# Gated attention and two feed-forward stages on one core: the first 384 tokens' feed-forward runs its first two steps before the second 384 tokens' attention begins

## The chip, the core and the metric

The kernel runs on one core of a Trainium2 chip. What is measured is device time in microseconds (us) from the start of the program to its end. The core has TensorE (PE in the profile) for matrix products, VectorE (DVE), ScalarE (ACT) and GpSimd (POOL) for work on tiles, and SyncE (SP), which here only issues DMA transfers. Each engine works through its own list of instructions in order and waits at an instruction until what that instruction needs is there.

## What is computed

A gated recurrence over 768 tokens (4 sequences, 8 heads of 48), then a product of two linear maps, then a choice of one of eight experts for each token:

```python
for t in range(S):                                   # attention
    state = alpha[:, :, t, :, None] * state + k_t v_t^T
    y[:, :, t] = q_t @ state
x = y as 3072 tokens x 384                           # first feed-forward stage ("moe")
x = ((x @ w_a) * (x @ w_b)) @ w_out                  # 384 -> 1536 -> 384
e = argmax(x @ w_gate + modality_bias[modality_id])  # second stage ("moe2")
out = gate(e) * (relu(x @ w1[e]) @ w2[e])            # 384 -> 1024 -> 384
```

All inputs but the modality ids are float64 or float32 with float32 accuracy wanted; the weights arrive as 64-bit numbers.

## The kernel before, in words

The 3072 tokens are cut into 8 groups of 384 (`WIN`), each of three chunks of 128. For each group `Attention` makes `xh[w]` and `xl[w]`: the attention output transposed and split into a high and a low part, so that a product is three fast passes on TensorE. `moe(w)` then takes the group through the first feed-forward stage in 12 steps f of 128 hidden columns: 9 products into `ab0` and 9 into `ab1` (L625), ScalarE copies the first (`asb`, L630), VectorE multiplies (`g`, L632), ScalarE and VectorE split it into `gh` (L634) and `gl` (L638), and one step later 9 products with `w_out` gather in three banks `px` (L616).

The weights come as 64-bit words and are turned into float32 parts by `convert`. They are loaded in six slices r = 0 to 5 (`load_weights(r)`: `wa`, `wb`, `wo`, each 768 KB, on SP's queue), and each slice serves two steps f. To convert one slice of one weight takes VectorE four instructions on 128x768 elements: L181, L184 and L188 put a float32 together in `cva`, `cvb` or `cvo`, then ScalarE writes the high part (L192) and VectorE the low part (L196) into `pa`, `pb` or `po`. `weights()` does them in the order a0, b0, o0, a1 and b1, o1, a2 and b2, and so on.

All this must happen beside the first group, since later groups use the converted weights again. So the beginning of the kernel is this: the attention of group 0 (`first`, an order written out by hand, with eight conversion instructions in it), then the 12 steps of `moe(0)`, and beside them the conversion of the slices and the attention of group 1 (`later`, `att1`). In this part the order on VectorE and SP is the program's order (`manual_schedule`), and the string `SEQ` says what that is: `r` is the next conversion step (one instruction of VectorE, with ScalarE's where there is one), `m` the first half of a step f, which ends with `gh`, `n` its second half with `gl` and the products of the step before, and `a` the next step of group 1's attention. Of these, `prepare(c)` has three: (1) the clamp of the turned alpha, a scan over it and a reciprocal (L370, L379, L382), (2) `kt` (L388), (3) a second scan and `qt` (L390, L392). Then come the scores (L404 on TensorE), the mask (L421, L422), `values` and `halves` (L452 to L479, with `xl` at L479), and the state's update (L509). TensorE, ScalarE and GpSimd take their order from a planner.

Turning (`turn`, L343) is a transpose of a raw tile on TensorE; alpha, k and q of a chunk are `raw_a`, `raw_k`, `raw_q`, loaded at L325. The turned tiles lie in three banks of PSUM until `prepare` has read them. On SP's queue group 1's first raw tiles go out ahead of `wo` of slice 0 and all of slice 1; a transfer waits until the eighth one before it has landed.

Of the kernel before, what the change touches and what calls it, by code (L numbers as in the profile page):

```python
# [29 lines left out]


SEQ = (
    "rrrmrrnaaarrrmrnrarra" "rrrmrrnaarrrmrnrarra" "rrrmrrnaarrrmrnrarra" "rrrmrrnaarrrmrnrarra" "rrrmrrnaarrrmrnrarr"
    "rrrmrnmnm"
)
WARM0, WARM1 = 7, (0, 3, 4, 0, 3, 0, 0, 0, 1)
# [8 lines left out]
def gla_moe_kernel(ctx, tc, q, k, v, alpha, w_a, w_b, w_out, modality_id, w_gate, modality_bias, w1, w2, out):  # L45
    nc = tc.nc
# [96 lines left out]
    words, parts, newest = {}, {}, {}  # L143
# [8 lines left out]
    def load_weights(r, names="abo"):  # L152

        for nm, w in (("a", w_a), ("b", w_b)):
            if nm not in names:
                continue
            words[nm, r] = new_w(f"w{nm}{r}", I32)


            heads = w.bitcast(I32)[:, r * 512 : (r + 1) * 512].rearrange("(h d) f -> h d f", h=H)  # L160
            for i in range(4):
                nc.sync.dma_start(  # L162
                    out=words[nm, r][32 * i : 32 * i + 32, : 2 * 512].rearrange("p (k f) -> p k f", k=2),
                    in_=heads[i::4, :32].rearrange("k d f -> d k f"),
                )
            nc.sync.dma_start(out=words[nm, r][:, 2 * 512 :], in_=heads[:, 32:])
        if "o" not in names:
            return
        words["o", r] = new_w(f"wo{r}", I32)
        newest["w"] = nc.sync.dma_start(  # L170
            out=words["o", r].rearrange("p (f d) -> p f d", f=2),
            in_=w_out.bitcast(I32)[r * 2 * P : (r + 1) * 2 * P, :].rearrange("(f p) d -> p f d", p=P),
        )
# [72 lines left out]
                    return  # L246
            yield

    def behind(steps):

        while True:
            with tc.issue_after(newest["mm"].ins):
                try:
                    next(steps)
                except StopIteration:
                    return
            yield
# [24 lines left out]
    class Attention:  # L282
# [206 lines left out]
        def carry(self, c):  # L489
            ktok = self.ktok.pop(c)  # L490
            pu = self.bank(f"u{self.w}_{c}")
            for p in range(NPAIR):
                nc.tensor.matmul(  # L493
                    pu[:, p * 96 : (p + 1) * 96],
                    ktok[:, p * P : (p + 1) * P],
                    self.vt[c][:, 2 * p : 2 * p + 2, :].rearrange("p h d -> p (h d)"),
                    start=True,
                    stop=True,
                )
            self.pu[c] = pu  # L500
# [277 lines left out]
    def small(name, shape, dt=F32):  # L778
        return m2.tile(shape, dt, bufs=1, name=name)
# [375 lines left out]
    def pipeline(y_d=None):  # L1155
        nonlocal ap, m2, fold, starts
        nc.vector.tensor_copy(base, eoff)
        with tc.tile_pool(name="att", bufs=1) as ap:
            if y_d is None:
                starts = ap.tile([P, NPAIR * P1], F32, name="starts")  # L1160
                nc.gpsimd.memset(starts, 0.0)

            def weights():
                yield from convert(0, "a", P)
                yield from convert(0, "b", P)
                for r in range(NF // 2):
                    o = convert(r, "o", DM)
                    yield from islice(o, 3)
                    ab = convert(r + 1, "ab", P) if r + 1 < NF // 2 else iter(())
                    yield from islice(ab, 1)  # L1170
                    yield from o
                    yield from ab

            if y_d is None:
                with tc.manual_schedule(engines={EN.DVE, EN.PE, EN.SP, EN.Activation}):
                    att0 = Attention(0, (nc.sync, nc.scalar))
                    for c, which in ((0, "akq"), (1, "akq"), (0, "v"), (2, "akq"), (1, "v"), (2, "v")):
                        att0.load(c, which)
                    rest = weights()
                    load_weights(0, "ab")  # L1180
                    later = Attention(1)

                    def second():
                        later.load(0, "akq")
                        load_weights(0, "o")
                        later.load(0, "v")
                        load_weights(1)

                    att0.first(rest, second)
                with tc.manual_schedule(engines={EN.DVE, EN.SP}):  # L1190
                    att1 = later.steps()
                    next(att1)
                    load_weights(2)
                    clear_table()
                    nc.sync.dma_start(out=wg_sb, in_=w_gate.rearrange("(k p) e -> p k e", p=P))
                    load_weights(3)
                    g0 = dict(r=rest, m=moe(0), a=att1)
                    f, done = 0, 8
                    g0["n"] = g0["m"]
                    for c in SEQ:  # L1200
                        if c == "m":
                            assert not (f < NF and ("b", f // 2) not in parts or f > 1 and ("o", f // 2 - 1) not in parts)
                            f += 1
                        done += c == "r"
                        if c == "r" and done == 14:
                            load_weights(4)
                            load_weights(5)
                        next(g0[c], None)
                    run((g0["m"], 1), (rest, 8), (att1, 1))
                    run((load_ids(), 1))  # L1210
                for w in range(1, NW - 1):
                    if w == 1:
                        with tc.issue_after(newest["mm"].ins):
                            turn_gate()
                        gate = gate_columns("gate", ap, 2, tag="cv", bufs=4)
                    att = Attention(w + 1)
                    run((after_first(att.steps()) if w == 1 else att.steps(), RATIO), (moe(w), 1), (route(w - 1, ap, gate if w > 2 else None), 1))
            else:
                for r in range(NF // 2):
                    load_weights(r)  # L1220
                clear_table()
                run((weights(), 1))
                for w in range(NW - 1):
                    x_from(w, y_d)
                    run((moe(w), 1))
                    if w < NW - 2:
                        run((route(w, ap), 1))
                x_from(NW - 1, y_d)
        with tc.tile_pool(name="m2", bufs=2) as m2:
            fold = small("fold", [P, TINY])  # L1230
            nc.vector.tensor_reduce(fold, ident.rearrange("p (j c) -> p c j", c=TINY), axis=AX.X, op=ALU.add)
            last = moe(NW - 1)
            gate = gate_columns("last", m2, 4, tag="wr", bufs=6) if y_d is None else None
            run((islice(last, 1), 1))
            early = []
            run((islice(last, MIX[0]), 1), (behind(chain(route(NW - 2, m2, gate), early_table(early))), 2))
            slots = [Slot(f"e{i}", "e", i, 2, (NW - 1) * WIN) for i in range(NEARLY)]
            for s_ in slots:
                s_.index()
            for s_ in slots[:2]:  # L1240
                s_.load()
            run((islice(last, MIX[1]), 1))
            if y_d is None:
                run((behind(spans()), 1))
            with tc.manual_schedule(engines=VECS):
                run((last, 1), (slots[0].split(), SPLIT), (behind(pause(MIX[2], slots[0].rows())), 1))

            big, tiny = [("l", i, 2) for i in range(NSB)], [("r", XSMALL + i, 1) for i in range(NTINY + XTINY)]
            order, rest = big[:NBIG], [big[NBIG:], [("r", i, 1) for i in range(XSMALL)], tiny[NTINY:]]
            riders = {}  # L1250
            if y_d is None:
                riders = {RIDE[n]: Tiny(f"t{n}", *tiny[n][:2], N) for n in range(NTINY)}
            else:
                order, rest = big + rest[1] + tiny, []
            slots += [Slot(f"l{n}", *o, N) for n, o in enumerate(order)]
            with nullcontext() if rest else tc.manual_schedule(engines={EN.SP}):
                puts = []
                go(slots, 1, (route(NW - 1, m2, puts=puts), early[0], puts), riders)
        return rest
# [108 lines left out]
    rest = pipeline()  # L1368
# [37 lines left out]
```

## Time and profile before

| what | us |
|---|---|
| median of 3 runs | 896.39 |
| lowest and highest of them | 895.86 and 898.45 |
| profiled execution, device time | 897.17 |
| its span, first to last instruction | 895.2 |
| VectorE busy in the span | 636.0 (71%) |
| TensorE busy in the span | 840.8 (94%) |

The profiled execution's own time is 0.78 us over the median. The share of the whole span says little here: the change touches only the stretch from some 25 us to 120 us after the start, in which VectorE is the busiest engine after TensorE. Times in the rows below are counted from the start of the span.

### The profile page before, as it was taken

How to read it: one execution, taken by the hardware profiler on the slowest of the kernel's cores; microseconds unless marked ns; L12 is line 12 of the kernel's file. 1: busy time of each engine (PE TensorE's matmuls, PEld its weight loads, DVE VectorE, ACT ScalarE, POOL GpSimd, SP SyncE). 2: the span in 40 equal slices, each digit the busy share in tenths (PEclk: the TensorE clock that was granted, in tenths of full speed). 3: DMA queues.
4: the chain of work that ended last, by engine and by line, in shares of the span. 5: the costliest groups of instructions: out<-in, count | busy, mean ns of one | idle time of the engine just before them, and what ended most of it. 6: DMA issues, size and time to landing. Idle time of an engine off the chain costs nothing.

```text
span 895.2 us, 16751 instructions
## 1 busy us (share of the span) xinstructions
PE 840.8 (94%) x6220; PEld 786.0 (88%) x6220; DVE 636.0 (71%) x1457; ACT 292.1 (33%) x681; POOL 199.5 (22%) x273
## 2 busy tenths in 40 slices
PE   7888889988997999999999999999699999999995
PEld 6677789978996999989899998999699999998994
DVE  7699889964595788499698676366369876775751
ACT  2223332212221222212122122122265555565541
POOL 5011101120011101011100100000425565455431
PEclk9889999998998999999999999999899999999998
DMA  9999846332234214023220000210580988695810
GB/s 170 200 197 199 181 123 207 93 62 68 63 77 74 81 28 106 27 63 96 41 78 10 1 28 1 71 28 1 202 299 24 361 289 310 191 358 186 281 60 22
DMA packets 124928, 110.98 MB, mean 124 GB/s; under 512 B 55759, under 2 KB 104051, under 8 KB 124836
## 3 DMA queue, kind: packets, MB, share of 16 engines
q1 hardware_dynamic: 114548, 99.00, 40.7%
q0 software_dynamic: 4032, 9.62, 3.1%
q10 hardware_dynamic: 6256, 1.19, 1.1%
q8 instruction: 51, 0.84, 0.4%
q14 instruction: 41, 0.34, 0.1%
HBM read 100.10 MB, written 9.82 MB: 123 GB/s over the span
## 4 chain that ended last, share of the span: by engine, by line
PE 65%; DVE 12%; DMA 10%; issue 6%; SPq 3%; POOL 2%; ACT 2%; POOLq 0%; DVEq 0%; ACTq 0%
PE ab L625 24%; PE px L616 12%; PE hl L1056 8%; PE pol L1004 8%; DMA wa<-in_moe_w_a 3%; PE he L1056 2%; PE s L404 2%; PE poe L1004 2%; DMA wb<-in_moe_w_b 2%; DMA tab_d<-rec,posi 2%; PE u L493 1%; DVE g L632 1%; DMA raw_a<-in_alpha 1%; SPq L162 1%; DVE at L358 1%
## 5 line engine op out<-in xcount | busy, mean ns | idle before, releaser
L625 PE MATMUL ab<-xh,pb 128*128 128x384 f32 x576 | 168.8, 346 | 16.3 <-DVE g L632 16.3
L625 PE MATMUL ab<-xh,pa 128*128 128x384 f32 x576 | 167.4, 344 | 9.7 <-ACT asb L630 7.3
L616 PE MATMUL px<-po,gh 128*128 128x384 f32 x576 | 139.5, 342 | 3.4 <-ACT gh L634 3.1
L634 ACT ACTIVATE gh<-g 128x384 fp32r<-128x384 f32 x96 | 50.3, 524 | 240.4 <-DVE g L632 234.4
L625 PEld LDWEIGHTS ab<-xh,pb 128*128 128x128 f32 x576 | 107.5, 191 | 21.4 <-DVE g L632 18.3
L625 PEld LDWEIGHTS ab<-xh,pa 128*128 128x128 f32 x576 | 106.2, 190 | 14.0 <-ACT asb L630 7.9
L632 DVE TENSOR_TENSOR g<-ab,asb 128x384 f32<-128x384 f32 x96 | 53.0, 552 | 81.5 <-PE ab L625 75.6
L616 PEld LDWEIGHTS px<-po,gh 128*128 128x128 f32 x576 | 104.3, 191 | 5.5 <-ACT gh L634 4.1
L625 PE MATMUL ab<-xl,pb 128*128 128x384 f32 x288 | 98.0, 340 | 0.0
L625 PE MATMUL ab<-xl,pa 128*128 128x384 f32 x288 | 97.4, 338 | 0.0
L630 ACT ACTIVATE asb<-ab 128x384 f32<-128x384 f32 x96 | 47.0, 490 | 147.8 <-PE ab L625 147.5
L616 PE MATMUL px<-po,gl 128*128 128x384 f32 x288 | 87.0, 341 | 0.0
L638 DVE TENSOR_TENSOR gl<-g,gh 128x384 fp32r<-128x384 f32 x96 | 56.2, 586 | 21.6 <-ACT gh L634 21.3
L392 POOL TENSOR_TENSOR qt<-qt,at 128x512 f32<-128x512 f32 x18 | 22.3, 1237 | 220.8 <-DVE qt L358 168.3
L1061 DVE SCALAR_TENSOR_TENSOR hll<-hl,hhl 128x256 fp32r<-128x256 f32 x72 | 30.3, 421 | 54.1 <-ACT hhl L1059 53.7
L671 DVE SCALAR_TENSOR_TENSOR junk<-xr,gate 128x384 bf16<-128x384 f32 x96 | 54.0, 562 | 4.8 <-ACT xr L648 3.2
L625 PEld LDWEIGHTS ab<-xl,pb 128*128 128x128 f32 x288 | 55.1, 191 | 0.1
L625 PEld LDWEIGHTS ab<-xl,pa 128*128 128x128 f32 x288 | 54.7, 190 | 0.1
L732 POOL DMA_INDIRECT tab_d<-rec,posi x24 | 24.2, 1010 | 135.7 <-DMA tab_d<-rec,posi 67.0
L616 PEld LDWEIGHTS px<-po,gl 128*128 128x128 f32 x288 | 52.9, 189 | 1.0 <-issue 0.6
L1059 ACT ACTIVATE hhl<-hl 128x256 fp32r<-128x256 f32 x72 | 27.7, 384 | 61.8 <-PE hl L1056 56.5
L437 POOL TENSOR_TENSOR state<-state,R 128x384 f32<-128x384 f32 x18 | 17.5, 971 | 131.2 <-DVE state L509 62.8
(332 smaller groups left out, 1860.0 us busy)
## 6 DMA issues: line engine op xcount, KB each, us to landing
w1rl<-in_moe_w SPq DMA_DIRECT2D x18, 768.0 KB, 8.1
w2rl<-in_moe_w SPq DMA_DIRECT2D x18, 768.0 KB, 4.9
raw_a<-in_alpha SPq DMA_DIRECT2D x72, 96.0 KB, 2.3
raw_k<-in_k SPq DMA_DIRECT2D x72, 96.0 KB, 2.3
raw_q<-in_q SPq DMA_DIRECT2D x72, 96.0 KB, 2.7
wo<-in_moe_w_out SPq DMA_DIRECT2D x6, 768.0 KB, 7.9
x_d<-xr SPq DMA_DIRECT2D x24, 192.0 KB, 2.1
w1re<-in_moe_w SPq DMA_DIRECT2D x6, 768.0 KB, 14.3
```

Source lines behind the costliest of these rows:

```text
L616: newest["mm"] = nc.tensor.matmul(px[t][:, :DM], a_, b_, start=(f == 0 and i == 0), stop=(f == NF - 1 and i == 2))
L625: nc.tensor.matmul(pt[:, :WIN], a_, b_, start=(n == 0), stop=(n == 3 * KD - 1))
L630: nc.scalar.activation(asb, pt[:, :WIN], AF.Copy)
L632: nc.vector.tensor_tensor(g, pab[1][:, :WIN], asb, op=ALU.mult)
L634: newest["act"] = nc.scalar.activation(gh, g, AF.Copy)
L638: newest["gl"] = nc.vector.tensor_tensor(gl, g, gh, op=ALU.subtract)
L671: nc.vector.scalar_tensor_tensor(junk, xr[w][t], 1.0, gate[e], op0=ALU.mult, op1=ALU.mult, accum_out=L[:, t, e : e + 1])
L732: put = nc.gpsimd.indirect_dma_start(out=tab_d[:, :], out_offset=bass.IndirectOffsetOnAxis(ap=posi[:, t : t + 1], axis=0), in_=rec[:, i, : ...
L1004: newest["mm"] = nc.tensor.matmul(self.po[t][:, :DM], a_, b_, start=(f == 0 and i == 0), stop=(f == NF2 - 1 and i == 2))
L1056: nc.tensor.matmul(pt[:, :n], a_, b_, start=(i == 0), stop=(i == 3 * KD - 1))
L1059: nc.scalar.activation(gh[:, :n], pt[:, :n], AF.Relu)
L1061: nc.vector.scalar_tensor_tensor(gl[:, :n], pt[:, :n], 0.0, gh[:, :n], op0=ALU.max, op1=ALU.subtract)
```

## The change

Three edits. `SEQ` gets a new first piece without any `a`: the first two steps f and the whole conversion of slice 1 (`a1`, `b1` and the first steps of `o1`) come before group 1's attention. The attention starts beside step f = 2; its later pieces hold a step more, so that it is through at the same place, step f = 9. `behind(att1, newest["first"])` makes the planner issue what belongs to group 1's attention behind the last state product of group 0 (L493, third chunk). And slices 4 and 5 are asked for in the program after the third `a` instead of the sixth `r`.

```diff
 SEQ = (
-    "rrrmrrnaaarrrmrnrarra" "rrrmrrnaarrrmrnrarra" ...
+    "rrrmrrnrrrmrnrrr" "rrrmrrnaaarrrmrnrarra" "rrrmrrnaarrrmrnrarra" ...
...
-    def behind(steps):
+    def behind(steps, ins=None):
         while True:
-            with tc.issue_after(newest["mm"].ins):
+            with tc.issue_after((ins or newest["mm"]).ins):
...
             for p in range(NPAIR):
-                nc.tensor.matmul(
+                newest["first"] = nc.tensor.matmul(
                     pu[:, p * 96 : (p + 1) * 96],
...
-                    g0 = dict(r=rest, m=moe(0), a=att1)
-                    f, done = 0, 8
+                    g0 = dict(r=rest, m=moe(0), a=behind(att1, newest["first"]))
+                    f, done = 0, 0
                     g0["n"] = g0["m"]
                     for c in SEQ:
...
-                        done += c == "r"
-                        if c == "r" and done == 14:
+                        next(g0[c], None)
+                        done += c == "a"
+                        if c == "a" and done == 3:
                             load_weights(4)
                             load_weights(5)
-                        next(g0[c], None)
```

The number of instructions stays; SP's list keeps its order. Three places show what moves. In the names the first number is the chunk or step and the last one is a serial number; `y_2` and `u_2` are group 0's third chunk, `pa_0`, `pk_0`, `pq_0` group 1's first turned tiles.

TensorE, end of group 0's attention, before:

```order
L236 MATMUL warm<-ones_b 128x256
L343 MATMUL pa_0_628<-ident,raw_a_0_363 128x128 x4
L343 MATMUL pk_0_641<-ident,raw_k_0_366 128x128 x4
L343 MATMUL pq_0_649<-ident,raw_q_0_369 128x128 x4
L452 MATMUL y_2_497<-qt_2_344,state 64x128 x4
L464 MATMUL y_2_497<-qt_2_344,state 32x128 x4
L468 MATMUL y_2_497<-sm_2_445,v_2_183 32x128 x8
L473 MATMUL y_2_497<-sm_2_445,vpad_116 32x128 x8
L493 MATMUL u_2_522<-v_2_183,ktok_2_443 128x96 x4
```

and after:

```order
L236 MATMUL warm<-ones_b 128x256
L452 MATMUL y_2_497<-qt_2_344,state 64x128 x4
L464 MATMUL y_2_497<-qt_2_344,state 32x128 x4
L468 MATMUL y_2_497<-sm_2_445,v_2_183 32x128 x8
L473 MATMUL y_2_497<-sm_2_445,vpad_116 32x128 x8
L493 MATMUL u_2_522<-v_2_183,ktok_2_443 128x96 x4
L343 MATMUL pa_0_723<-ident,raw_a_0_363 128x128 x4
L343 MATMUL pk_0_736<-ident,raw_k_0_366 128x128 x4
L343 MATMUL pq_0_744<-ident,raw_q_0_369 128x128 x4
```

The three turnings have moved behind the last products of group 0's attention.

VectorE, between the first step f and the conversion of slice 1 (`cva_622`, `cvb_623`), before:

```order
L196 TENSOR_TENSOR po_590<-cvo_586,po_590 128x2x384
L638 TENSOR_TENSOR gl_0_621<-g_0_617,gh_0_619 128x384
L370 TENSOR_SCALAR at_0_627<-pa_0_628 128x4x128
L376 MEMSET R_0_635 128x2
L378 MEMSET starts 128x4
L379 SCALAR_TENSOR_TENSOR R_0_635<-at_0_627,starts 128x516
L382 RECIPROCAL starts<-R_0_635 128x4
L388 TENSOR_TENSOR kt_0_640<-pk_0_641,R_0_635 128x512
L390 SCALAR_TENSOR_TENSOR at_0_627<-at_0_627,starts 128x516
L392 TENSOR_TENSOR qt_0_648<-pq_0_649,at_0_627 128x512
L181 TENSOR_SCALAR cvb_623<-wb_382 128x768
L184 SCALAR_TENSOR_TENSOR cva_622<-wa_376,cva_622 128x768
```

and after:

```order
L196 TENSOR_TENSOR po_590<-cvo_586,po_590 128x2x384
L638 TENSOR_TENSOR gl_0_621<-g_0_617,gh_0_619 128x384
L181 TENSOR_SCALAR cvb_623<-wb_382 128x768
L184 SCALAR_TENSOR_TENSOR cva_622<-wa_376,cva_622 128x768
L184 SCALAR_TENSOR_TENSOR cvb_623<-wb_382,cvb_623 128x768
L632 TENSOR_TENSOR g_1_652<-ab_1_1_642,asb_1_640 128x384
L188 SCALAR_TENSOR_TENSOR cva_622<-wa_376,cva_622 128x768
L638 TENSOR_TENSOR gl_1_656<-g_1_652,gh_1_654 128x384
```

The eight instructions of `prepare(0)` have left this place (they now stand behind `gl_2`), and the conversion that reads `wb` of slice 1 follows `gl_0` directly.

VectorE, where group 1's first chunk is split (`xl_198<-y_0`), before:

```order
L188 SCALAR_TENSOR_TENSOR cvb_799<-wb_560,cvb_799 128x768
L390 SCALAR_TENSOR_TENSOR at_1_752<-at_1_752,starts 128x516
L392 TENSOR_TENSOR qt_1_872<-pq_1_873,at_1_752 128x512
L196 TENSOR_TENSOR pa_856<-cva_798,pa_856 128x6x128
L196 TENSOR_TENSOR pb_869<-cvb_799,pb_869 128x6x128
L479 TENSOR_TENSOR xl_198<-y_0_884,xh_197 128x3x128
```

and after:

```order
L188 SCALAR_TENSOR_TENSOR cvb_894<-wb_578,cvb_894 128x768
L479 TENSOR_TENSOR xl_198<-y_0_977,xh_197 128x3x128
L196 TENSOR_TENSOR pa_959<-cva_893,pa_959 128x6x128
L196 TENSOR_TENSOR pb_972<-cvb_894,pb_972 128x6x128
L509 TENSOR_TENSOR state<-u_0_1013,state 64x4x32
```

`xl` of the first chunk now follows the last of the joins (L188) at once; four instructions that stood between them are elsewhere. From `xl` of the third chunk on, in step f = 9, both lists are the same.

## Rows read from the trace of the kernel before

**Rows 1.** The page's head: span of the profiled execution.
```profile
span 895.2 us, 16751 instructions
```

**Rows 2.** Busy time by stretch; us, busy us of PE, PEld, DVE, ACT, POOL, clock, DMA share.
```profile
28.99:34.78 5.79, 5.34 (x57) 3.89 (x56) 0.00 (x1) 0.49 (x1) 0.00 (x0) 0.50 1.05 262
...
41.12:49.49 8.37, 3.79 (x18) 2.99 (x18) 6.96 (x12) 1.64 (x3) 0.83 (x1) 0.97 1.04 196
49.49:61.59 12.10, 11.86 (x81) 10.48 (x82) 11.89 (x19) 3.57 (x6) 2.40 (x3) 0.74 0.90 203
61.59:119.53 57.94, 51.16 (x388) 45.14 (x388) 52.84 (x81) 22.30 (x42) 5.55 (x8) 1.00 0.88 193
...
130.00:170.00 40.00, 39.52 (x286) 36.77 (x288) 37.41 (x78) 10.72 (x27) 4.95 (x7) 1.00 0.55 160
```

**Rows 3.** VectorE in order of time: start, length, instruction, [idle before it, its releaser].
```profile
34.78 0.56 DVE L479 TENSOR_TENSOR xl<-y,xh 128x384 fp32r<-128x384 f32 x1 [5.79 <-ACT xh L478]
...
36.12 0.55 DVE L181 TENSOR_SCALAR cvo<-wo 128x768 int32<-128x768 int32 x1
...
41.12 0.56 DVE L632 TENSOR_TENSOR g<-ab,asb 128x384 f32<-128x384 f32 x1 [0.83 <-PE ab L625]
...
43.39 0.96 DVE L196 TENSOR_TENSOR po<-cvo,po 128x768 fp32r<-128x768 f32 x1 [1.24 <-ACT po L192]
...
44.73 0.68 DVE L370 TENSOR_SCALAR at<-pa 128x512 f32<-128x512 f32 x1
...
49.49 0.55 DVE L181 TENSOR_SCALAR cvb<-wb 128x768 int32<-128x768 int32 x1
...
53.50 1.39 DVE L188 SCALAR_TENSOR_TENSOR cvb<-wb,cvb 128x768 int32<-128x768 int32 x1
...
56.98 0.68 DVE L370 TENSOR_SCALAR at<-pa 128x512 f32<-128x512 f32 x1
...
59.15 0.53 DVE L181 TENSOR_SCALAR cvo<-wo 128x768 int32<-128x768 int32 x1
...
61.59 0.55 DVE L632 TENSOR_TENSOR g<-ab,asb 128x384 f32<-128x384 f32 x1
```

**Rows 4.** Transfer of `wo`, slice 0, issued at 29.32: KB, us to landing.
```profile
wo<-in_moe_w_out SPq DMA_DIRECT2D x1, 768.0 KB, 5.9
```

**Rows 5.** The chain that ended last, in order of time: start, length, what.
```profile
38.19 7.76 DMA wb<-in_moe_w_b
...
45.97 3.53 DMA wb<-in_moe_w_b
49.50 0.55 DVE cvb L181
...
52.85 2.29 PE px L616 x6
...
56.90 3.15 PE ab L625 x18
```

**Rows 6.** TensorE in order of time, around its gap at 46 to 49 us.
```profile
45.03 0.69 PE L616 MATMUL px<-po,gl 128*128 128x384 f32 x3
49.63 2.08 PE L404 MATMUL s<-qt,kt 64*128 64x128 f32 x16 [3.91 <-DVE qt L392]
```

**Rows 7.** TensorE alone by stretch: us, busy us (instructions), granted clock, DMA share.
```profile
43.50:49.60 6.10, 2.02 (x10) 0.95 1.03 195
49.60:55.80 6.20, 6.07 (x30) 0.50 0.82 190
```

**Rows 8.** VectorE's four waits of over 0.25 us between 62 and 120 us.
```profile
78.33 0.96 DVE L196 TENSOR_TENSOR po<-cvo,po 128x768 fp32r<-128x768 f32 x1 [0.88 <-ACT po L192]
...
101.29 0.67 DVE L638 TENSOR_TENSOR gl<-g,gh 128x384 fp32r<-128x384 f32 x1 [0.31 <-ACT gh L634]
...
104.79 0.56 DVE L479 TENSOR_TENSOR xl<-y,xh 128x384 fp32r<-128x384 f32 x1 [1.96 <-ACT xh L478]
...
119.53 0.56 DVE L479 TENSOR_TENSOR xl<-y,xh 128x384 fp32r<-128x384 f32 x1 [1.29 <-ACT xh L478]
```

More of the change, by code (lines that the diff above doesn't have):

```diff
@@ L32 @@
 SEQ = (
-    "rrrmrrnaaarrrmrnrarra" "rrrmrrnaarrrmrnrarra" "rrrmrrnaarrrmrnrarra" "rrrmrrnaarrrmrnrarra" "rrrmrrnaarrrmrnrarr"
+    "rrrmrrnrrrmrnrrr" "rrrmrrnaaarrrmrnrarra" "rrrmrrnaaarrrmrnrarra" "rrrmrrnaaarrrmrnrarra" "rrrmrrnaaarrrmrnraarra"
     "rrrmrnmnm"
```

## The prediction

> **What bounds the kernel now.** I read the busy time by stretch first, then VectorE's own order of time, then the chain of waits. The page's head gives the span [rows 1]; the profiled execution took 897.17 us, 0.78 us over the median, so I make the sum on 897.17 and take 0.78 off at the end. The edits touch the stretch from about 29 to 120 us. From 61.59 to 119.53 us VectorE is busy 52.84 of 57.94 us and TensorE 51.16 [rows 2]: VectorE has hardly any slack there, and what reaches its list late stays late. Its order from `xl` of the third chunk on (119.53) is that of before, and behind it, from 130 to 170 us, TensorE is busy 39.52 of 40 us and VectorE 37.41 [rows 2], so a delay at 119.53 is carried to the end one to one. The sum is therefore VectorE's lateness at that point.
>
> Ahead of 61.59 VectorE loses time at three places. From 28.99 to 34.78 it waits 5.79 us for `xh`, since TensorE stood at the turnings for raw tiles still on their way and then worked at half clock [rows 2, 3]. It waits 0.83 us before `g` at 41.12 and 1.24 us before `po` at 43.39 [rows 3]. These are what the change could win. From 44.73 to 61.59 it has no idle time: `prepare(0)` (44.73 to 49.49), the conversion of `wb` and `wa` with step 1 (49.49 to 56.98), the first part of `prepare(1)` (56.98 to 59.15), three instructions on `cvo` (59.15 to 61.59) [rows 3].
>
> **Part 1: the turnings behind the products.** TensorE no longer stands at the turnings, so `xl` can begin up to 5.79 us earlier, at 28.99 [rows 3]. What stood between its start and `cvo` L181 took 36.12 - 34.78 = 1.34 us, so VectorE is at `cvo` L181 by 30.3. But this instruction reads `wo` of slice 0, issued at 29.32, landing 5.9 us later, at 35.2 [rows 4]. The transfers do not move: SP's order is the same, its issues wait for earlier landings and not for the engines, and the DMA share in these stretches is 0.90 to 1.05 [rows 2]. So of 5.79 us only 36.12 - 35.2 = 0.9 us is won here; `g_0` and `po` follow some 0.9 us earlier, or up to 0.83 more if the wait for TensorE shrinks too [rows 3].
>
> **Part 2: conversion of slice 1 ahead of prepare(0).** Before, `prepare(0)` began at 44.73 when `gl_0` was through [rows 3]; now `cvb` L181 stands there, ready about 43.8 (44.73 less 0.9). It reads `wb` of slice 1. The last piece of that was issued at 38.19, and the chain shows SP's next issue released 7.76 us later, at 45.95, by this landing [rows 5]. VectorE so sits idle some 2.2 us to 45.95. Everything else in its list is the same work in another order, so the lateness is 45.95 - 44.73 = **+1.2 us**. Bounds: the wait before `cvb` is not in the trace; the landing may come half a microsecond to either side, 0.7 to 1.7. `prepare(0)`'s 4.76 us, which covered this transfer, no longer does. `prepare`'s own cost is not changed, nor that of the instruction that runs longer beside a GpSimd mask (1.39 us at 53.50 [rows 3]): it goes elsewhere with the mask, counted at nothing; at best it is saved, about 0.4 us.
>
> **Part 3: TensorE's clock.** In the trace TensorE ends `px` at 45.72, idles 3.91 us for `qt` and then runs at a granted clock of 0.50 (1.2 GHz) from 49.60 to 55.80, against 0.95 in the stretch with the gap [rows 6, 7]. That cost nothing, since VectorE had 12 us of work by itself. After the change the gap lies in the same place and what follows it is on the path. `px` ends about 44.8 (0.9 earlier). In the chain `px` of step 1 follows `cvb` L181 by 52.85 - 49.50 = 3.35 us, by way of `g_1` and `gh_1` [rows 5], so it now starts at 45.95 + 3.35 = 49.3. The gap is 4.5 us, longer than 3.91, so I expect half clock again for about 6.2 us, to 55.5. Step 1's nine products at 2.29 us for six [rows 5] take 3.4 us, to 52.7. Then the 18 products `ab_2`: 3.15 us at full clock [rows 5], but to 55.5 only 1.4 us of that is done; the rest ends at 57.25. VectorE wants `g_2` after nine instructions from `cvb` on (49.49 to 56.98, 7.5 us, less at most 0.9 for slow ones [rows 3]) and three on `cvo` (2.44 us [rows 3]): 45.95 + 6.6 + 2.44 = 55.0. So it stalls 2.25 us. With TensorE at full clock all the while there is no stall: `px` takes 1.7 us, and `ab_2` can end by 54.7, its last nine waiting for `pb`. Where in the stretch the clock comes back is not fixed by these rows (55.80 is the latest at which it did), so between 0 and 2.25 I take **+1.6**, nearer to the row.
>
> The Trainium skill, in "TensorE: Matmul & The Clock Gate", section "Part 1: The HAM clock gate", says that the low clock is the default and that sustained work must lift it each time after idleness. That speaks against this change, which lengthens an idle time and puts the products that pay for it on the path; rows 6 and 7 agree with it (a gap of 3.91 us, then 0.50). By this rule the sum is as given; without it the sum would lack the 1.6.
>
> **Part 4: the waits of the later pieces.** VectorE's waits from 61.59 to 119.53 are 0.88 + 0.31 + 1.96 + 1.29 = 4.44 us [rows 8]. Now `xl` of the first chunk follows L188 at once, which is the pattern of the wait at 119.53: 1.3 us. `xl` of the second chunk stands behind a `gl` of 0.55 us instead: 1.96 - 0.55 = 1.4. The third stays, 1.3. The waits of 0.88 and 0.31 were behind ScalarE's masks of group 1, which have moved; I count them as gone. Together 4.0 instead of 4.44: **-0.4 us**. Bounds: all but the third vanish and the stall of `po` too, -1.5 (about half of the 3.15 us that could go); or the two return and a wait like 1.96 is added, +2.
>
> **Part 5: slices 4 and 5, and instruction counts.** The two loads are asked for at another place of the program, but SP's list keeps its order and TensorE, VectorE and ScalarE execute the same instructions: 0. What hides it is that SP waits for landings anyway.
>
> **Sum.** 1.2 + 1.6 - 0.4 = +2.4 us: 899.6 on the profiled execution, **898.8** on the median scale. Lowest terms together: 0.7 + 0 - 1.5 = -0.8 (895.6); highest: 1.7 + 2.25 + 2 = +6 (902.4).
>
> **The rivals.**
> - A second stretch at half clock (slower). `prepare(0)` now runs after `gl_2`; TensorE may again idle while VectorE does its 4.76 us, and then the scores (2.08 us at half clock [rows 6]), turnings and products of two steps run slow on the path. Against it: TensorE has step 3's 18 products, which need nothing new, to fill with. It decides if TensorE idles there for something like the 3.91 us of rows 6. Price: a further stall of the size of part 3's 2.25 and a bit, about 2.6, so +5: 901.4.
> - The chain itself names a transfer of `wb` as what released `cvb` L181 at 49.50 [rows 5]. If that was true, the wait lasts 3.5 us longer and the time is 902.3. Against it: VectorE was busy without a break to 49.49 [rows 3], and the piece named was issued at 45.97, behind all of slice 1.
> - No stall of `g_2` (no change): the clock is back in time, or the gap is filled. +1.2 - 0.4 = +0.8: 897.2.
> - The weights land earlier (faster): raw tiles or weights come in another time than in the trace, and VectorE waits neither at `cvo` (4.9 us) nor at `cvb` (2.2). Then the 5.79 us of rows 3 is kept but for some 1.5 us, by which the waits of `g` and `po` (0.83 and 1.24 now) could grow: -4.3, so 892.1. Against it: a full DMA queue that the change doesn't touch.
>
> **How the numbers follow.** About 0.3%, 2.7 us, is what a measurement of this kernel can tell from no change: faster is below 893.7, slower above 899.1. My forecast (897.4 to 900.6) has 0.48, of which 0.20 lies above 899.1. The second half-clock stretch 0.18, the late `wb` 0.05, no stall 0.20 (0.01 of it faster), early weights 0.09 (0.08 faster). So faster 0.09, same 0.28 + 0.19 + 0.01 = 0.48, slower 0.20 + 0.18 + 0.05 = 0.43. The range 895.8 to 902.0 leaves out the early weights, the late `wb`, and tails.
>
> **What would show it.** In the profile after: VectorE idle some 4 to 5 us before `cvo` L181 at 35 and 2 to 3 us before `cvb` L181 at 46, both released by DMA (part 1 and 2); clock 0.50 from about 49 to 55 and a wait of `g` for `ab` L625 of 1 to 2 us near 55 to 57 (part 3); waits of 1.3 to 1.4 us before each `xl` (part 4); the third `xl` at 120 to 123 instead of 119.53. I am wrong if `cvb` begins well before 45.9, if TensorE works through 44 to 49, or if VectorE's waits from 62 to 120 come to less than 3 or more than 6 us.

## The result and the profile after

The changed kernel takes 902.21 us (median of 8 runs, 900.12 to 904.29) against 896.92 us (8 runs) before: ratio 1.0059, 95% interval 1.0043 to 1.0076. It is slower, by 0.59%. The forecast was 898.8 with a range to 902.0; the time lies just above the range. The profiled execution took 901.7 us, 4.5 us more than that of before.

VectorE of after in order of time, the rows that answer to [rows 3] and [rows 8]:

```profile
35.07 0.56 DVE L181 TENSOR_SCALAR cvo<-wo 128x768 int32<-128x768 int32 x1 [4.28 <-DMA wo<-in_moe_w_out]
...
42.14 0.56 DVE L181 TENSOR_SCALAR cva<-wa 128x768 int32<-128x768 int32 x1 [2.30 <-issue]
...
47.48 0.56 DVE L181 TENSOR_SCALAR cvb<-wb 128x768 int32<-128x768 int32 x1 [3.44 <-DMA wb<-in_moe_w_b]
...
57.23 0.56 DVE L632 TENSOR_TENSOR g<-ab,asb 128x384 f32<-128x384 f32 x1 [0.46 <-PE ab L625]
...
67.98 0.69 DVE L638 TENSOR_TENSOR gl<-g,gh 128x384 fp32r<-128x384 f32 x1 [0.22 <-ACT gh L634]
...
88.43 0.56 DVE L479 TENSOR_TENSOR xl<-y,xh 128x384 fp32r<-128x384 f32 x1 [2.30 <-ACT xh L478]
...
115.40 0.56 DVE L479 TENSOR_TENSOR xl<-y,xh 128x384 fp32r<-128x384 f32 x1 [2.23 <-ACT xh L478]
...
124.14 0.56 DVE L479 TENSOR_TENSOR xl<-y,xh 128x384 fp32r<-128x384 f32 x1 [1.29 <-ACT xh L478]
```

The 5.79 us at 34.78 are gone, and in their place stand 4.28 us for `wo`, as part 1 said. VectorE then waits 2.30 us before `cva`, where [rows 3] has 0.83 and 1.24 us before `g` and `po`, and 3.44 us before `cvb` for `wb`. For the 2.30 us the view names no releaser; SP's issue of the next piece of `wa`, held back until an earlier transfer has landed, starts 0.16 us before `cva`, and in the eight other traces with such a wait the two lie 0.16 or 0.17 us apart, so most likely VectorE waits there for the landing of `wa`. The three `xl` of group 1 wait 5.82 us together, where [rows 8] has 3.25 for the second and third and none for the first. The third `xl` starts at 124.14 instead of 119.53: 4.61 us late, and the execution is 4.53 us longer. So close an agreement is partly luck: in the eleven traces of kernels whose order from the third `xl` on is that of before, what follows its start takes 775.9 to 780.1 us. The stretch up to the third `xl` can be read to some tenths of a microsecond from a trace, the whole execution cannot.

TensorE in order of time, and its granted clock by stretch (columns as in [rows 2]), the answers to [rows 6] and [rows 7]:

```profile
44.26 0.70 PE L616 MATMUL px<-po,gl 128*128 128x384 f32 x3
50.85 2.29 PE L616 MATMUL px<-po,gh 128*128 128x384 f32 x6 [5.89 <-ACT gh L634]
...
64.37 2.08 PE L404 MATMUL s<-qt,kt 64*128 64x128 f32 x16 [2.56 <-DVE qt L392]
...
84.54 2.29 PE L616 MATMUL px<-po,gh 128*128 128x384 f32 x6 [0.55 <-ACT gh L634]
```

```profile
44.90:50.90 6.00, 0.11 (x2) 0.05 (x1) 3.42 (x5) 0.52 (x1) 0.00 (x0) 0.67 0.97 170
50.90:53.90 3.00, 3.00 (x10) 3.00 (x11) 2.96 (x5) 1.69 (x2) 0.00 (x0) 0.52 0.64 185
53.90:57.30 3.40, 3.40 (x21) 3.40 (x20) 2.87 (x5) 0.92 (x2) 0.00 (x0) 1.00 0.83 199
```

```profile
64.00:68.00 4.00, 3.63 (x26) 3.43 (x27) 3.78 (x7) 1.55 (x4) 1.27 (x2) 0.57 0.84 178
...
84.00:88.00 4.00, 3.46 (x23) 2.60 (x24) 2.13 (x3) 2.93 (x7) 1.30 (x1) 0.57 1.04 207
```

TensorE idles 5.89 us, and the clock falls while it idles (0.67 on average from 44.9 to 50.9). The products behind the gap run at 0.52 (1.2 GHz), but only for 3 us: at 53.9 the clock is back, `ab_2` runs at 1.00 (2.4 GHz), and `g` waits 0.46 us. Two more stretches at half clock follow, at 64 to 68 behind a gap of 2.56 us, and at 84 to 88; before has 1.00 in both places. In the second, six products of `px` take 2.29 us and stand ahead of the last products of `y`, for whose `xh` the first `xl` waits.

The chain that ended last, followed back from the second `xl` of after, shows what that one waits for:

```profile
104.92 0.63 PE k L485 x4
105.54 2.87 PE ab L625 x16
108.42 0.86 PE u L493 x8
109.28 1.09 PE s L404 x8
110.36 3.35 PE ab L625 x18
...
114.23 0.62 PE y L473 x16
```

From `k` to `y` TensorE works without a gap at full clock, with 34 products `ab` of two steps ahead of the products that VectorE is waiting for. So this wait comes from TensorE's order and amount of work: VectorE reaches `xl` before TensorE has reached `y`.

### The profile page after: what moved, and what is told of

It is laid out like the page before. It is cut to its first block, busy times and chain, and to the rows that moved or that the text cites. A ratio compares the mean times of both kernels' runs of the same rounds, so it can differ in the third digit from the quotient of the medians.

```text
span 899.7 us, 16753 instructions
## 1 busy us (share of the span) xinstructions
PE 840.5 (93%) x6220; PEld 787.4 (88%) x6220; DVE 635.0 (71%) x1457; ACT 292.2 (32%) x681; POOL 202.1 (22%) x273
## 4 chain that ended last, share of the span: by engine, by line
PE 67%; DVE 15%; DMA 8%; issue 5%; POOL 1%; SPq 1%; ACT 1%; DVEq 0%; POOLq 0%; ACTq 0%
PE ab L625 25%; PE px L616 11%; PE hl L1056 9%; PE pol L1004 8%; DMA wa<-in_moe_w_a 4%; PE s L404 2%; PE he L1056 2%; PE poe L1004 2%; DMA tab_d<-rec,posi 2%; DVE R L379 1%; DVE at L390 1%; DVE g L632 1%; PE u L493 1%; DVE gl L638 1%; DVE at L358 1%
```

## Experiments

All ratios are against before, in runs on the same chip; they are the ratios on record with their 95% intervals, and not exactly the quotients of the medians. Times of single executions scatter: the runs of one kernel lie some 4 to 8 us apart, so a trace says where the time lies and the ratios say how much. In the three sets below before itself had medians of 897.68, 898.08 and 897.76 us. In the edits `...` stands for what is left out. The third piece of the new string is `rrrmrrnaaarrrmrnrarra`, with three `a` in a row, as the edits below have it; the excerpt under "The change" has two.

**The turnings alone.** Before with the edit of `behind`; `SEQ` and the loads as before:

```diff
...
-                    g0 = dict(r=rest, m=moe(0), a=att1)
+                    g0 = dict(r=rest, m=moe(0), a=behind(att1, newest["first"]))
```

> Before with one edit: group 1's first work is planned behind the last state product of group 0 (the turnings move); the order string and the place of the loads stay as before. Theory A (cover): the loss of 4.6 us comes from VectorE's wait for wb of slice 1 (3.44 us) and from later waits for xh, and both hang on the string; so here the start is about 1 us earlier (cvo L181 at 35.1 instead of 36.1), prepare(0) still covers the landing of wb, and the time is 0.5 to 1.2 us under before, about 896.0. Theory B (the turnings): group 1's turnings in their new place delay TensorE; then this kernel is slower than before by 1 us or more.

Measured: 898.75 us, ratio 1.0002 (0.9986 to 1.0018). The turnings don't bring the loss of after (theory B): the interval ends at 1.0018, and after has 1.0059. The small gain of theory A, 0.5 to 1.2 us, doesn't show either, though the interval (from 0.9986) does not exclude it. VectorE of this kernel, then TensorE's clock from 104 to 108 us in this kernel and in before:

```profile
36.21 0.56 DVE L181 TENSOR_SCALAR cvo<-wo 128x768 int32<-128x768 int32 x1 [5.44 <-DMA wo<-in_moe_w_out]
...
106.83 0.56 DVE L479 TENSOR_TENSOR xl<-y,xh 128x384 fp32r<-128x384 f32 x1 [3.89 <-ACT xh L478]
```

```profile
104.00:108.00 4.00, 4.00 (x26) 3.15 (x25) 1.17 (x2) 0.98 (x2) 0.63 (x1) 0.50 0.53 142
```

```profile
104.00:108.00 4.00, 3.02 (x17) 2.70 (x17) 3.17 (x8) 0.97 (x3) 0.64 (x1) 1.00 0.70 185
```

`wo` landed at 36.2 here, so even the 0.9 us of part 1 was not there. In this part the two kernels run the same instructions on TensorE in the same order, from 77 to 101 us within 0.2 us of each other, and yet one execution then goes on at full clock and the other at half. With it the second `xl` waits 3.89 us instead of 1.96. So these instructions alone don't settle whether a stretch runs at half clock, and what does is not shown; where `xl` stands close behind its products, it cost some 2 us here.

**The string alone.** After without the edit of `behind`:

```diff
-                    g0 = dict(r=rest, m=moe(0), a=behind(att1, newest["first"]))
+                    g0 = dict(r=rest, m=moe(0), a=att1)
```

> After without the one edit: the new string, but the turnings stand where they stood before, ahead of group 0's last products. Theory A: VectorE waits for wb whether it comes there 1 us earlier or later, so the time is that of after, 902.2, within 0.7 us. Theory B: the whole loss hangs on the turnings, and the time is near before, 897.

Measured: 901.09 us, ratio 1.0035 (1.0018 to 1.0052). VectorE:

```profile
45.80 0.56 DVE L181 TENSOR_SCALAR cvb<-wb 128x768 int32<-128x768 int32 x1 [0.78 <-DMA wb<-in_moe_w_b]
```

The string brings the loss. Its start is a microsecond later, and this only shortens the wait for `wb`. The median is 1.1 us under after, a little more than expected. In this execution `wb` was there at 45.8, 1.7 us earlier than in after.

**The gap filled.** After with 28 products on constants ahead of step 0's `px`:

```diff
                 second(*gprev)
+            if w == 0 and f == 1:
+                warm(14)
             gprev = (f, gh, gl)
```

> After with 28 idle products of 256 columns on TensorE ahead of the products of step 0 with w_out, to fill its gap of 5.89 us (44.96 to 50.85). Theory A: VectorE waits for data there and not for TensorE; only the 0.46 us before g of step 2 can go, so 901.5 to 902.5. Theory B' (the clock): the half clock after the gap is what costs; with it gone the time falls by 1.5 us or more, under 900.7.

Measured: 901.82 us, ratio 1.0037 (1.0023 to 1.0051). VectorE:

```profile
46.70 0.56 DVE L181 TENSOR_SCALAR cvb<-wb 128x768 int32<-128x768 int32 x1 [2.90 <-DMA wb<-in_moe_w_b]
...
56.71 0.56 DVE L632 TENSOR_TENSOR g<-ab,asb 128x384 f32<-128x384 f32 x1 [0.72 <-PE ab L625]
...
86.69 0.56 DVE L479 TENSOR_TENSOR xl<-y,xh 128x384 fp32r<-128x384 f32 x1 [1.29 <-ACT xh L478]
...
114.82 0.56 DVE L479 TENSOR_TENSOR xl<-y,xh 128x384 fp32r<-128x384 f32 x1 [3.42 <-ACT xh L478]
```

TensorE behind the filled gap:

```profile
50.08 1.77 PE L616 MATMUL px<-po,gh 128*128 128x384 f32 x6 [2.33 <-ACT gh L634]
```

The gap shrank from 5.89 to 2.33 us, the time stayed. But the half clock did not go with the gap: from 50.5 to 54.5 us TensorE worked at 0.57, and `g` of step 2 waited 0.72 us, more than the 0.46 in after. So this run doesn't show what the clock behind the gap, my part 3, costs. What bounds that cost is the wait of this `g`: 0 to 1.74 us in the nine traces with the new string or a variant of it. Further on a half-clock stretch sat at 100 to 108 us this time (0.74 and 0.83), and with it the long wait moved from the first `xl` (1.29 now) to the second (3.42).

**Slice 1 first.** After with `wo` of slice 0 and slice 1 ahead of group 1's raw tiles on SP's queue, and with group 1's first turnings behind the products `ab` of step 2, since their tiles now land later:

```diff
-                        later.load(0, "akq")
                         load_weights(0, "o")
-                        later.load(0, "v")
                         load_weights(1)
+                        later.load(0, "akq")
+                        later.load(0, "v")
...
-                loaded[w, c, nm] = self.queue().dma_start(out=r[:, :, :D], in_=rows)
+                with tc.issue_after(newest["w"].ins) if w == 1 else nullcontext():
+                    loaded[w, c, nm] = self.queue().dma_start(out=r[:, :, :D], in_=rows)
...
-                        next(g0[c], None)
+                        with tc.issue_after(newest["ab"].ins) if c == "a" and done < 3 else nullcontext():
+                            next(g0[c], None)
```

> After with the transfers in another order: wo of slice 0 and all of slice 1 go out ahead of group 1's raw tiles (six of them and a v stood ahead or between), and the first turnings stand behind the products of step 2, since their tiles land later. Theory A: wo lands 3 to 5 us earlier and wb of slice 1 at 41 to 44 instead of 47.4; VectorE's waits before cvo (4.28 us) and cvb (3.44 us) shrink together by 4 to 6 us, and the time is 3 to 5 us under after: 897 to 899. Theory C (the later waits for xh and TensorE's clock set the time, the start doesn't matter): within 1 us of after.

Measured: 903.41 us (7 runs), ratio 1.0049 (1.0026 to 1.0071). No gain. VectorE (the code's lines are one higher here):

```profile
31.93 0.56 DVE L181 TENSOR_SCALAR cvo<-wo 128x768 int32<-128x768 int32 x1 [3.52 <-DMA wo<-in_moe_w_out]
...
54.10 0.56 DVE L633 TENSOR_TENSOR g<-ab,asb 128x384 f32<-128x384 f32 x1 [0.83 <-PE ab L626]
56.80 0.56 DVE L181 TENSOR_SCALAR cva<-wa 128x768 int32<-128x768 int32 x1 [2.15 <-DMA wb<-in_moe_w_b]
...
116.28 0.56 DVE L480 TENSOR_TENSOR xl<-y,xh 128x384 fp32r<-128x384 f32 x1 [3.40 <-ACT xh L479]
```

`cvb` waits for nothing, and `g` of step 2 starts 3.1 us earlier than in after (54.10 against 57.23). Right behind it 2.15 us are given back, since the raw tiles now stand ahead of slice 2, and the rest goes into a wait of 0.68 us before a `gl` and the waits for `xh` (1.97, 3.40 and 1.29 us). Theory A had the first half right and not the second. Theory C, that a better start is lost again further on, stands for this kernel.

**The cover put back.** After with `prepare(0)` ahead of the conversion that reads `wb`:

```diff
-    "rrrmrrnrrrmrnrrr" "rrrmrrnaaarrrmrnrarra" ...
+    "rrrmrrnaaarrrmrnrrr" "rrrmrrnrrrmrnrarra" ...
```

> After with one move in the string: prepare(0) of group 1 stands again between gl of step 0 and the conversion that reads wb of slice 1; the rest of the attention stays where after has it. Theory A (cover): VectorE does its 4.76 us of prepare(0) while wb lands, the 3.44 us wait before cvb is gone, and the time falls by 2 to 3.5 us against after, to 898.5 to 900. Theory C (TensorE sets the later part): the gain comes back as longer waits for xh further on, and the time stays within 1 us of after, 901 to 903.

Measured: 902.22 us, ratio 1.0045 (1.0022 to 1.0068), inside what theory C expected. The profiled execution was the fastest of its twelve (899.07 us). VectorE:

```profile
43.77 0.68 DVE L370 TENSOR_SCALAR at<-pa 128x512 f32<-128x512 f32 x1
...
59.10 0.56 DVE L632 TENSOR_TENSOR g<-ab,asb 128x384 f32<-128x384 f32 x1 [0.61 <-PE ab L625]
...
86.61 0.56 DVE L479 TENSOR_TENSOR xl<-y,xh 128x384 fp32r<-128x384 f32 x1 [3.41 <-ACT xh L478]
...
113.56 0.56 DVE L479 TENSOR_TENSOR xl<-y,xh 128x384 fp32r<-128x384 f32 x1 [2.22 <-ACT xh L478]
...
123.18 0.56 DVE L479 TENSOR_TENSOR xl<-y,xh 128x384 fp32r<-128x384 f32 x1 [2.17 <-ACT xh L478]
```

No wait is left before `cvb`. With `prepare(0)`'s 4.76 us taken off, `g` of step 2 is 2.9 us earlier than in after (54.34 against 57.23). At the third `xl` only 0.96 us of that is left; the three waits have grown from 5.82 to 7.80 us. So covering the transfer alone buys nothing that can be measured.

**The three `xl` later.** After with each `xl` of group 1 behind two joins or three conversions that stood right behind it:

```diff
-    ... "rrrmrrnaaarrrmrnrarra" "rrrmrrnaaarrrmrnrarra" "rrrmrrnaaarrrmrnraarra"
+    ... "rrrmrrnaaarrrmrnrrraa" "rrrmrrnaaarrrmrnrarra" "rrrmrrnrrraaamrnrarraa"
```

> After with xl of group 1's three chunks moved on VectorE's list behind two or three conversion instructions that stood right behind it; nothing else of the string is changed. Theory A: the waits for xh (2.30, 2.23 and 1.29 us in after) shrink to under 2 us together and the time falls by 2.5 to 4 us, to 898 to 899.7. Theory C: TensorE is itself late there, so the wait reappears before the next g (ab late) or gl, and the time stays within 1 us of after.

Measured: 896.9 us, ratio 0.9996 (0.9976 to 1.0017). The profiled execution was the fastest of its twelve (893.68 us). VectorE:

```profile
45.72 0.56 DVE L181 TENSOR_SCALAR cvb<-wb 128x768 int32<-128x768 int32 x1 [3.03 <-DMA wb<-in_moe_w_b]
...
86.72 0.56 DVE L479 TENSOR_TENSOR xl<-y,xh 128x384 fp32r<-128x384 f32 x1
...
112.63 0.55 DVE L479 TENSOR_TENSOR xl<-y,xh 128x384 fp32r<-128x384 f32 x1
...
119.30 0.55 DVE L479 TENSOR_TENSOR xl<-y,xh 128x384 fp32r<-128x384 f32 x1
```

All three waits are gone, and little of them comes back (a new wait of 0.60 us before one `g`); the wait for `wb` is still there. The time is that of before. Theory C falls for this place: TensorE was late only for `xl`, and two or three other instructions cover it. It doesn't follow that the places of `xl` are all of the loss: before itself has 3.25 us of such waits [rows 8], and these are out of this kernel too. The next run gives the fair comparison.

**The same remedy in the kernel before.** Second and third `xl` behind the two joins:

```diff
-    ... "rrrmrrnaarrrmrnrarra" "rrrmrrnaarrrmrnrarr"
+    ... "rrrmrrnaarrrmrnrrraa" "rrrmrrnaarrrmrnrrra"
```

> Before with xl of the second and third chunk moved on VectorE's list behind the two joins (pa, pb) that stood right behind it. Theory A: the waits of 1.96 and 1.29 us go for the most part, 1.5 to 3 us under before. Theory C: within 1 us of before.

Measured: 893.49 us, ratio 0.9952 (0.9931 to 0.9972). This beats both kernels. VectorE of this kernel, and of the second trace of before:

```profile
104.09 0.56 DVE L479 TENSOR_TENSOR xl<-y,xh 128x384 fp32r<-128x384 f32 x1
...
117.57 0.55 DVE L479 TENSOR_TENSOR xl<-y,xh 128x384 fp32r<-128x384 f32 x1
```

```profile
103.92 0.56 DVE L479 TENSOR_TENSOR xl<-y,xh 128x384 fp32r<-128x384 f32 x1 [1.96 <-ACT xh L478]
...
118.63 0.56 DVE L479 TENSOR_TENSOR xl<-y,xh 128x384 fp32r<-128x384 f32 x1 [1.29 <-ACT xh L478]
```

The waits of 1.96 and 1.29 us are gone. The gain, 4.3 us at a ratio of 0.9952 (2.5 to 6.2 us by its interval), agrees with their 3.25 us. Waits that only some executions have, as 3.89 us in the first experiment, would go too, but that is argued and not shown.

Against this kernel the one above, in which no `xl` of group 1 waits either, is slower: 0.9996 to 0.9952, with intervals that just miss each other (from 0.9976, and to 0.9972), 3.4 us by the medians. So with the waits of `xl` out of both, the rest of the new order still loses time. The start is where its trace shows new waits: 3.03 us for `wb`, 0.60 us before `g` of step 2.

**Second traces.** Before and after, unchanged:

> Before, unchanged, for a second trace. If the landing of wb of slice 1 is settled by the queue alone, the transfer behind it on the same semaphore is released at 45.95 us again, within 0.3; if the clock between 62 and 124 us is settled by the order of the instructions alone, it is 1.00 throughout again. If either differs, what after lost there is in part chance of one execution.

> After, unchanged, for a second trace and beside the others on one chip. Theory E: VectorE waits again for wb (over 2 us) and for xh three times (over 5 us together), whichever stretch TensorE runs at half clock; 901 to 903.

Measured: before 896.55 us, ratio 0.9995 (0.997 to 1.002), with the rows above: the two waits of `xl` in [rows 8] to a hundredth and full clock from 60 to 124 us, but the next transfer on `wb`'s semaphore released at 46.90 us, not 45.95. After 902.38 us, ratio 1.0048 (1.0028 to 1.0067). VectorE of after's second trace:

```profile
47.31 0.56 DVE L181 TENSOR_SCALAR cvb<-wb 128x768 int32<-128x768 int32 x1 [3.55 <-DMA wb<-in_moe_w_b]
...
58.35 0.56 DVE L632 TENSOR_TENSOR g<-ab,asb 128x384 f32<-128x384 f32 x1 [1.74 <-PE ab L625]
...
88.10 0.56 DVE L479 TENSOR_TENSOR xl<-y,xh 128x384 fp32r<-128x384 f32 x1 [1.29 <-ACT xh L478]
...
115.03 0.56 DVE L479 TENSOR_TENSOR xl<-y,xh 128x384 fp32r<-128x384 f32 x1 [2.20 <-ACT xh L478]
...
124.51 0.56 DVE L479 TENSOR_TENSOR xl<-y,xh 128x384 fp32r<-128x384 f32 x1 [2.04 <-ACT xh L478]
```

The same waits at the same places, with other shares: `g` of step 2 waits 1.74 us instead of 0.46, the first `xl` 1.29 instead of 2.30, the third 2.04 instead of 1.29.

**The first `xl` alone, both ways.** Before with one step more of the attention ahead of step 3, so that its first `xl` stands directly behind L188 as in after, and after with its first `xl` alone behind the joins:

```diff
-    "rrrmrrnaaarrrmrnrarra" "rrrmrrnaarrrmrnrarra" ...
+    "rrrmrrnaaarrrmrnrarra" "rrrmrrnaaarrrmrnrarr" ...
```

```diff
-    "rrrmrrnrrrmrnrrr" "rrrmrrnaaarrrmrnrarra" "rrrmrrnaaarrrmrnrarra" ...
+    "rrrmrrnrrrmrnrrr" "rrrmrrnaaarrrmrnrarra" "rrrmrrnaaarrrmrnrrraa" ...
```

> Before with one piece of the string as after has it: one step of the attention more ahead of step 3, so that xl of the first chunk follows the last L188 at once (the two joins and qt no longer stand between). Theory E: a wait for xh of 1.3 to 2.3 us appears there, and the time rises by 1 to 2.5 us, to 898 to 900. Rival (the place of the first xl costs nothing, the loss of after is all at its start): within 0.5 us of before.

> After with xl of the first chunk alone moved behind the two joins. Theory E: the wait of 2.30 us there goes, the time falls by 1 to 2.3 us, to 900 to 901. If the wait comes back in full at the second xl (2.23 us in after), within 0.5 us of after.

Measured: 901.14 us for the first, ratio 1.0031 (1.0013 to 1.005), and 900.39 us for the second, ratio 1.0027 (1.001 to 1.0043). VectorE of the one and of the other:

```profile
75.36 0.56 DVE L479 TENSOR_TENSOR xl<-y,xh 128x384 fp32r<-128x384 f32 x1 [1.97 <-ACT xh L478]
```

```profile
88.44 0.55 DVE L479 TENSOR_TENSOR xl<-y,xh 128x384 fp32r<-128x384 f32 x1
...
113.63 0.56 DVE L479 TENSOR_TENSOR xl<-y,xh 128x384 fp32r<-128x384 f32 x1 [2.22 <-ACT xh L478]
```

The wait of 1.97 us came with the clock at 1.00 from 60 to 92 us; with the new place also came a wait of 1.29 us before a `gl`, and the second `xl` waits 1.29 us instead of 1.96. A kernel that has nothing of the new start, but the new place of the first `xl`, is slower by 0.31% (0.13 to 0.5%): by the middle values this piece alone costs about half of what after loses. Taken out of after, it gives 2.0 us back (902.38 to 900.39 in one set); these two intervals overlap, so that number is not sure by itself.

**Both remedies.** After with the cover put back and the three `xl` later:

```diff
-    "rrrmrrnrrrmrnrrr" "rrrmrrnaaarrrmrnrarra" "rrrmrrnaaarrrmrnrarra" "rrrmrrnaaarrrmrnrarra" "rrrmrrnaaarrrmrnraarra"
+    "rrrmrrnaaarrrmrnrrr" "rrrmrrnrrrmrnrarra" "rrrmrrnaaarrrmrnrrraa" "rrrmrrnaaarrrmrnrarra" "rrrmrrnrrraaamrnrarraa"
```

> After with both remedies: prepare(0) back ahead of the conversion that reads wb, and xl of the three chunks behind the conversions or joins. Theory E (two causes: 1. VectorE waits at the start for wb and then for ab of step 2, 2. xl stands too close behind its products): this kernel loses nothing against tail_shift, so it measures 892.5 to 895. If only the second cause counts, it is no faster than xh_later, 896 to 898.

Measured: 896.37 us, ratio 0.9974 (0.9957 to 0.9992). The median lies where only the second cause would count (896 to 898); by the ratio, 895.4 us, it lies between the two expectations, so this run does not decide. Against the three `xl` alone (0.9996) the cover would be worth 0.22%, 2 us, but the intervals overlap. It does not reach 0.9952, and there the intervals overlap as well. The profiled execution was the slowest of its twelve (901.43 us). VectorE's first `xl` and the clock around it:

```profile
89.04 0.56 DVE L479 TENSOR_TENSOR xl<-y,xh 128x384 fp32r<-128x384 f32 x1 [1.80 <-ACT xh L478]
```

```profile
84.00:88.00 4.00, 4.00 (x28) 3.18 (x26) 3.19 (x4) 1.67 (x3) 0.09 (x1) 0.50 1.08 197
```

At half clock even the later `xl` can wait; in the run with the three `xl` later, at 0.70 in the same stretch, it did not.

## Why the prediction was wrong, step by step

| VectorE's lateness, us | forecast | after | after, second trace |
|---|---|---|---|
| `cvb` against `prepare(0)` at 44.73 (part 2) | +1.2 | +2.75 | +2.58 |
| wait of `g_2` (part 3) | +1.6 | +0.46 | +1.74 |
| later waits less 4.44 (part 4) | -0.4 | +1.60 | +1.09 |
| sum | +2.4 | +4.81 | +5.41 |
| third `xl` less 119.53, measured | | +4.61 | +4.98 |
| profiled device time | 899.6 | 901.7 | 903.82 |

Up to the third `xl` the sum closes to 0.2 and 0.4 us, so no term is missing; two had the wrong size, part 2 and part 4. From there on it does not close as well: the second trace is 4.98 us late at the third `xl` and ends 6.65 us later than the profiled execution of before.

**Part 1 was right** in its mechanism: the 5.79 us turned into a wait for `wo` at 35.07, and the gain of about 1 us is swallowed by the next transfers: VectorE is ready for `cvb` 0.69 us earlier than [rows 3] has it at this place (44.04 against 44.73) and waits there for `wb`. The turnings alone change nothing that can be measured (1.0002).

**Part 2 failed by size.** The wait, its place and its releaser were as forecast. The landing was taken from one row of one execution (45.95) with half a microsecond to either side. The six traces in which `cvb` waited for it start it at 45.72, 45.80, 46.70, 46.99, 47.31 and 47.48: mean 46.67, so +1.9 would have been fair, with 1 us to either side. The rival that the chain named (49.50) didn't come.

**Part 3 was right on the gap and the half clock, within its bounds on the stall** (0.46 and 1.74 in 0 to 2.25). Its reading of [rows 7] was too simple: it let the half clock begin with the work. In after's first trace the clock had fallen well inside the gap, and only 3 us of work ran at half clock; in the second it fell late in the gap (0.87 over the 4.55 us), the products behind it ran at 0.50 from 50.7 to 56.3 us, and `g` waited 1.74 us. So it is in part luck that 1.6 lies between the two.

**Part 4 is the step that failed.** I priced the first `xl` by its nearest row (1.29), took the second as 0.55 us shorter than in before, and counted two other waits as gone. The two were gone. But the second `xl` waited 2.23 and 2.20 us instead of 1.4, and 2.20 to 2.23 in all five traces in which it has after's place and full clock ahead of it (after twice, the string alone, the cover put back, the first `xl` alone). The `gl` ahead of it did not shorten its wait: by the chain above TensorE has 34 products of `ab` to do before it comes to `y`, and I had counted as if `y` came when it did in before. In after's two traces the first and the third `xl` waited 1.29 us, as priced, where TensorE was at full clock ahead of them; where it was not, they waited 2.30 us (the first in the first trace, 0.57) and 2.04 us (the third in the second trace, 0.65 from 120 to 124 us). So at full clock the three waits come to 4.8 us instead of 4.0, and half clock ahead of an `xl`, for which part 4 had no term, added 1.0 and 0.75 us. All waits behind `g_2` up to the third `xl` came to 6.04 us, just past the 6 that I had named as a sign of being wrong, and to 5.53 us in the second trace. The upper bound of +2 held the term, but its value was on the wrong side of zero.

How much of the loss belongs to which cause is shown only in part. The places of `xl` cost time: 1.0031 for one of them alone in before. The rest of the new order costs time as well: 0.9996 against 0.9952 when no `xl` waits in either kernel. What the uncovered `wb` costs of this is between nothing (cover alone) and 2 us (cover on top of the later `xl`), and stays open.

**The rivals.** The one that I gave 0.18 came nearest (901.4), and its first half happened: TensorE idled 2.56 us before the scores and ran at 0.57. But there it cost VectorE 0.22 us, not 2.6. What cost was half clock further on, where `xl` stood waiting; so its number was near for another reason. The rival with early weights (892.1) did not come, and it would not have paid: even with slice 1's transfers first and no wait before `cvb`, the time stayed (1.0049).

## What to carry to other kernels

When work is pulled closer together on a busy engine's list, look for the instruction that waits for a chain through other engines (here `y`, `xh`, `xl`), and leave it as many independent instructions behind its producer as the wait is long; two joins of 0.95 us there gained 0.48%, while 5.79 us of idle time taken away at the start gained nothing. Work that stands over a transfer can be its cover even if nothing in the trace waits for that transfer (3.44 us of wait appeared when it was moved, though putting it back alone gained nothing that could be measured), and a landing read from one execution should be given the scatter of several. An engine that starts earlier only gains what the next wait on its list leaves.

## What was not expected of the hardware

The same transfer, in a queue issued in the same order, was there at times 1.8 us apart (45.72 to 47.48, counted from the start of the span) from one execution and kernel to the next. And TensorE's clock fell to 0.50 in one kernel and stayed at 1.00 in another on the same row of instructions (the turnings alone and before): up to 101 us both had just run transposes, small products and two gaps of 0.75 us.

Among the five traces with the old string (before twice, the turnings alone, the two shifts of `xl`) one has such a stretch between 60 and 124 us. All nine with the new string or a variant of it have at least one, eight of them between 60 and 72 us. So the new order brings such stretches, though not always to the same place; in the prediction this rival had 0.18. The Trainium skill, "TensorE: Matmul & The Clock Gate", section "Part 1: The HAM clock gate", says that how many products run at the low clock when a kernel starts differs from run to run of the same kernel. The traces show such a difference in the middle of a kernel as well: after's two executions have 0.57 and 1.00 from 84 to 88 us.
